# Keys and values as nine rows on 64 partitions, two heads side by side, in a linear-attention and SoLU kernel

## The chip, the cores and the metric

One core of one Trainium2 chip runs the whole program. The metric is the device time of one execution in microseconds (us), the median over several runs. Of the core's engines the text uses short names: PE (TensorE, matrix products), DVE (VectorE), ACT (ScalarE), POOL (GpSimd) and SP (SyncE, whose queue issues every load, store and DMA transpose of this kernel). PSUM is the memory into which PE writes; it has eight banks of 512 float32 columns on 128 partitions.

## What is computed

q, k and v have the shape (8, 8, 576, 64): batches, heads, rows, columns, all float32. Attention is linear: the softmax of q runs along its 64 columns, the softmax of k along the 576 rows.

```python
q_s = softmax(q, axis=-1)                  # along the 64 columns
k_s = softmax(k, axis=2)                   # along the 576 rows
kv  = einsum('bhsd,bhse->bhde', k_s, v)    # 64 x 64 for each head
x   = einsum('bhsd,bhde->bhse', q_s, kv)   # then to (4608, 512)
h   = x @ w_in                             # w_in 512 x 1024
solu = h * softmax(h)
ln  = (solu - mean) / sqrt(var + 1e-6) * g_ln
out = ln @ w_out                           # w_out 1024 x 512
```

w_in, w_out and g_ln come as float64, two 32-bit words a number, and are turned into float32 on the chip. The maximum and the sum in the softmax of k run over rows, and rows lie on partitions; that is why the maxima take a detour over PE, below.

## The kernel before

**Steps and the order list.** The program is a set of Python generators, each of which issues the instructions of one piece of work up to its next `yield`. The string ORDER names the generators one after the other; each name runs one step. `K3*2` is two steps of the keys of batch 3; `.v` puts that step's movable instruction on DVE instead of its usual engine. An engine carries out its instructions in the order in which they were issued, so the list fixes the order on each engine, and on SP's queue the order of the loads. The names: LQ, LK and LV load q, k and the remaining rows of v; V loads and copies a quarter of a batch's v (`V02`: batch 0, quarter 2); K is the keys; Qa, Qb, Qc and R are the softmax of q and its transposes; S a scale; x, h and o are, for each of 36 row tiles of 128 rows, attention, the first and the second product of the feed-forward part; w and y decode the weights; W and Z scale them into two float16 parts; LG loads g_ln; P issues four products whose result nobody reads.

**Row tiles.** A batch's 576 rows are 4 x 128 "main" rows, laid as (p c) with four neighbouring rows on one partition, and 64 "rest" rows. The rest rows of an even batch lie on partitions 0 to 63 and those of the odd batch after it on 64 to 127, and for q two batches share one tile for them.

**Keys (generator `keys`, L354 to L428).** For a batch, `km` holds the main rows of k as [128, 8 heads, 4, 64] and `kr` the rest as [64 of 128, 8 heads, 64]. DVE takes the maxima over the four rows of a partition in two halves of the heads (L365, L367) and joins kr to them (L370). `tops_of` turns the [128, 512] result with four PE transposes into `turned` (L341), reduces it on DVE to a column (L344), spreads the column with four PE transposes into `wide` (L348), and ACT copies that to `kb` (L351). Then kb is subtracted from km in two halves (L376, on POOL or DVE) and from kr (L381), and ACT takes exponentials (L378, L383). PE multiplies: for each pair of heads and each of the four rows two products of 128 rows, 64 columns of weights and 65 moving columns (L395), and 16 products of 64 rows for the rest (L400). The 65th column of v is all ones, so it gives the softmax's denominator. The two heads of a pair write the two halves of the output's partitions, all in one PSUM bank, `kv`. DVE divides (L403 to L407) and takes the largest value (L409), which PE and DVE spread over the partitions (L173, L176), and ACT and DVE write the scaled float16 high and low parts into `bd` (L422 to L426).

**Attention and feed-forward.** `attend` (L529) multiplies bd by the transposed softmax of q, and ACT and DVE copy x out as two float16 parts (L541, L543). `hidden` makes 24 products (L566) into two PSUM banks, and DVE, ACT and POOL work on them for the SoLU and the normalisation (L573 to L622); `project` makes 24 products (L640) for a row tile and copies them out (L648, L650).

**PSUM.** The tag `h` has two places of two banks, `o` one bank, and `att` three banks. turned, wide, kv, x and, in the last six row tiles, every second o take turns in `att`.

**v.** `load_v` loads two heads, [128, 2, 4, 64], and copies them into `vm` beside the ones (ACT, or DVE with `.v`); the rest rows are loaded straight into `vr`. **g_ln** is loaded with one number to a packet, as [128, 8] (L295).

Of the kernel before, what the change touches and what calls it, by code (L numbers as in the profile page):

```python
# [760 lines left out]
```

## Time and profile before

| what | value |
|---|---|
| median of 3 runs | 469.29 us (468.37 to 469.74) |
| profiled execution | 468.76 us, its span 467.0 us |
| granted clock of PE, mean | 0.996 |
| busy: PE, DVE, ACT, POOL | 439.9, 349.9, 282.4, 200.0 us |
| o products L640 | 888 |
| h products L566 | 840 |
| products of k and v, L395 and L400 | 512 and 128 |
| loads of km, kr, vr for one batch, issue to landing | 7.1, 6.2, 4.8 us (medians) |
| DMA packets | 159240, of them 127840 under 512 bytes |

How to read it: a "span" is from the first to the last instruction; the profiled execution's own time is 1.8 us longer. A row of a timeline names start, length, engine, line, operation, output<-inputs, shapes and count. A product's recorded length includes its way through the array, and neighbours overlap, so what a run of products takes is read from its first start to the next one's. A row of groups gives count, busy time, mean length in ns, and the idle time of the engine ahead of it. A row of waits gives who waited for whom, the sum, the number and the longest.

### The profile page before, as it was taken

What the parts mean: (1) busy time and instruction counts of PE and PEld (TensorE: products, weight loads), DVE (VectorE), ACT (ScalarE), POOL (GpSimd) and SP (SyncE); (2) the same over time, 40 slices, a digit from 0 to 9 for tenths busy, and PEclk for the clock granted to TensorE, in tenths of its full rate; (3) what the DMA queues carried; (4) which work ended last, traced back from release to release, by engine and by line L of the source; (5) the groups of instructions that cost most, each with busy time, mean ns of one, the idle gap of its engine ahead of it and who ended that gap; (6) DMA issues with size and microseconds to landing.
All of it is one profiled execution on the core that took longest, in us unless ns stands there. A gap on an engine that the chain in (4) does not pass through costs nothing.

```text
span 467.0 us, 8294 instructions
## 1 busy us (share of the span) xinstructions
PE 439.9 (94%) x3142; PEld 221.4 (47%) x3142; DVE 349.9 (75%) x620; ACT 282.4 (60%) x469; POOL 200.0 (43%) x286
## 2 busy tenths in 40 slices
PE   0678889999999999999999999999999999999997
PEld 0334344455546454545454455445545445444445
DVE  4989999998987889879789788668877844633500
ACT  1789899777658657466667448654764454522401
POOL 4123966577159356314665322735364421211200
PEclk9989999999999999999999999999999999999999
DMA  8999989589593997598757973869324673232522
GB/s 251 311 316 303 208 190 214 104 215 207 152 237 72 219 231 159 146 193 212 146 126 210 226 141 63 226 146 201 71 67 46 135 163 54 60 70 71 133 63 67
DMA packets 159240, 74.99 MB, mean 161 GB/s; under 512 B 127840, under 2 KB 152672, under 8 KB 159200
## 3 DMA queue, kind: packets, MB, share of 16 engines
q1 hardware_dynamic: 159200, 74.47, 69.0%
q8 instruction: 24, 0.39, 0.4%
q14 instruction: 16, 0.13, 0.1%
HBM read 36.70 MB, written 9.44 MB: 99 GB/s over the span
## 4 chain that ended last, share of the span: by engine, by line
PE 86%; DVE 6%; POOL 3%; ACT 3%; DMA 1%; issue 1%; SPq 0%; POOLq 0%; ACTq 0%; DVEq 0%
PE o L640 40%; PE h L566 36%; PE x L529 3%; PE kv L395 3%; PE warm_up L696 1%; DMA qm<-in_q_dram 1%; PE kv L400 1%; DVE wi L289 1%; DVE qnmx L443 1%; POOL qm L445 1%; PE turned L341 1%; PE wide L348 1%; DVE iw L262 1%; POOL km L376 1%; DVE km L376 0%
## 5 line engine op out<-in xcount | busy, mean ns | idle before, releaser
L640 PE MATMUL o<-wo,uT 128*128 128x512 f16 (+1 forms) x888 | 197.4, 373 | 0.0
L566 PE MATMUL h<-wi,xT 128*128 128x512 f16 x840 | 193.1, 379 | 2.7 <-ACT e L609 2.3
L640 PEld LDWEIGHTS <-uT 128*128 128x128 f16 x888 | 86.2, 98 | 97.8 <-issue 0.3
L566 PEld LDWEIGHTS <-xT 128*128 128x128 f16 x840 | 81.5, 98 | 98.8 <-issue 3.0
L573 DVE TENSOR_REDUCE top<-h 128x1 f32<-128x1024 f32 x36 | 43.9, 1221 | 24.9 <-PE h L566 24.7
L602 DVE SCALAR_TENSOR_TENSOR u<-h,nmu,u 128x1024 f16<-128x1024 f32 x36 | 46.0, 1277 | 16.7 <-ACT u L600 16.5
L609 ACT ACTIVATE e<-h,nmu 128x1024 f32<-128x1024 f32 x36 | 40.1, 1113 | 22.1 <-DVE u L602 22.1
L595 DVE SCALAR_TENSOR_TENSOR h<-h,ph,e 128x1024 f32<-128x1024 f32 x36 | 46.3, 1287 | 5.5 <-POOL ph L592 4.0
L589 POOL TENSOR_TENSOR p<-pi,mone 128x1 f32<-128x1 f32 x36 | 25.9, 718 | 49.5 <-DVE pi L586 42.7
L600 ACT ACTIVATE u<-h,nmu 128x1024 f16<-128x1024 f32 x36 | 40.0, 1112 | 0.8
L579 ACT ACTIVATE e<-h,nm,hs 128x1024 f32<-128x1024 f32 x31 | 37.2, 1201 | 0.7
L597 ACT ACTIVATE nmu<-s 128x1 f32<-128x1 f32 x36 | 7.3, 202 | 49.4 <-DVE h L595 49.3
L445 POOL TENSOR_TENSOR qm<-qm,qnmx 128x1024 f32<-128x1024 f32 (+1 forms) x14 | 25.7, 1844 | 21.7 <-DVE qnmx L443 14.6
L650 ACT ACTIVATE os<-o,rr 128x512 f32<-128x512 f32 (+1 forms) x23 | 15.3, 667 | 31.1 <-PE o L640 24.4
L622 POOL TENSOR_TENSOR r<-var,mhalf 128x1 f32<-128x1 f32 x36 | 24.2, 675 | 22.5 <-DVE var L619 22.0
L461 POOL TENSOR_TENSOR qhl<-qm,qhl 128x1024 f16<-128x1024 f32 (+1 forms) x11 | 22.5, 2041 | 19.4 <-DVE qhl L163 10.3
L575 ACT ACTIVATE nm<-top,hs 128x1 f32<-128x1 f32 x31 | 9.1, 294 | 35.2 <-DVE top L573 35.0
L456 POOL TENSOR_TENSOR qm<-qm,qrec 128x1024 f32<-128x1024 f32 (+1 forms) x11 | 20.7, 1879 | 19.2 <-DVE qrec L454 19.1
L543 DVE SCALAR_TENSOR_TENSOR xT<-x,xT 128x512 f16<-128x512 f32 x35 | 23.6, 683 | 5.2 <-ACT xT L541 5.1
L586 POOL TENSOR_SCALAR pi<-am 128x1 f32<-128x1 f32 x19 | 7.5, 393 | 41.8 <-DVE am L583 41.1
L443 DVE TENSOR_REDUCE qnmx<-qm 128x16 f32<-128x1024 f32 (+1 forms) x17 | 19.3, 1147 | 6.0 <-DMA qm<-in_q_dram 6.0
L541 ACT ACTIVATE xT<-x 128x512 f16<-128x512 f32 x35 | 20.0, 590 | 5.9 <-PE x L529 5.8
(139 smaller groups left out, 547.4 us busy)
## 6 DMA issues: line engine op xcount, KB each, us to landing
v<-in_v_dram SPq DMA_DIRECT2D x32, 256.0 KB, 3.7
out_dram<-os SPq DMA_DIRECT2D x31, 256.0 KB, 3.4
km<-in_k_dram SPq DMA_DIRECT2D x7, 1024.0 KB, 7.1
qm<-in_q_dram SPq DMA_DIRECT2D x7, 1024.0 KB, 6.8
w_in<-in_moe_w_in_dram SPq DMA_DIRECT2D x8, 512.0 KB, 6.9
w_out<-in_moe_w_out_dram SPq DMA_DIRECT2D x8, 512.0 KB, 5.6
out_dram<-os SPq DMA_DIRECT2D x10, 128.0 KB, 2.7
qm<-in_q_dram SPq DMA_DIRECT2D x2, 512.0 KB, 4.4
```

The source lines that it names most:

```text
L443: nc.vector.tensor_reduce(shaped(nmx), x, axis=AX.X, op=ALU.max, negate=True)
L445: on(nc.gpsimd).tensor_tensor(x, x, wide(nmx), op=ALU.add)
L566: nc.tensor.matmul(h[:, ns], xT[:, t, kc], wi[:, s, kc, ns], start=(i == 0), stop=(i == len(terms) - 1))
L573: nc.vector.tensor_reduce(top, h, axis=AX.X, op=ALU.max, negate=True)
L579: nc.scalar.activation(e, h, AF.Exp, bias=nm, scale=hs, accum_out=z)
L589: nc.gpsimd.tensor_tensor(p, pi, mone, op=ALU.pow)
L595: nc.vector.scalar_tensor_tensor(h, h, ph, e, op0=ALU.mult, op1=ALU.mult, accum_out=s1)
L600: nc.scalar.activation(u[:, 0], h, AF.Identity, bias=nmu)
L602: nc.vector.scalar_tensor_tensor(u[:, 1], h, nmu, u[:, 0], op0=ALU.add, op1=ALU.subtract)
L609: nc.scalar.activation(e, h, AF.Square, bias=nmu, accum_out=s2)
L622: nc.gpsimd.tensor_tensor(r, var, mhalf, op=ALU.pow)
L640: nc.tensor.matmul(o, uT[:, j, f], wo[:, s, f, cols], start=(f == 0 and j == 0 and s == 0), stop=(f == NF - 1 and j == 1))
```

## The change

k and v are no longer split into main and rest rows. A head's 576 rows lie as nine rows on each of 64 partitions, and an even and an odd head lie beside each other on the two halves of the 128 partitions; for one pair of heads that is one run of [128, 9 x 64] numbers, 2304 bytes to a partition. The loads of kr and vr (the generators LV) go.

The maxima over the nine rows take three steps on DVE (rows 0 to 3 with 4 to 7, then pairs, then the last pair and the ninth row), for batch 0 in two parts, for the others at once. turned and wide are two transposes each; the reduction gives one maximum for each head half, and a new copy (`cols`) spreads it over 64 columns before the second transpose. The subtraction and the exponential run in two parts of [128, 2, 9, 64]. The products are 72 of 64 rows by 64 weight columns by 65 moving columns, in fours that cover the four quarters of the array, and the two row halves write two PSUM banks of the tag `att`. The denominators and the division take two instructions each. The heads' places in `bd` move from pairs (n j) to (i n). g_ln is loaded as eight rows of 128 numbers and turned on PE. A batch's K has 24 steps instead of 28 (batch 0: 27), and P has 9 instead of 11. ORDER is another list throughout, and `.v` stands at other steps; its text is left out here but for the places that the prediction speaks of.

```diff
@@ ORDER
-    "LQ0*2 Q0a*2 LK0*3 Q0b.v Q0c.v Q0a.v Q0b V03 K0.v w3 Q0a w3 K0 Q0a.v Q0a K0*2 Q0b V03 Q0c.v*2 V00 w0 "
-    "K0 w3 Q0b.v K0 w0 Q0a.v K0*2 LV0 P V02.v V00 K0 w3 V01 Q0a P w3 K0.v w0 K0 K0.v w2 w0 V02 w2 w0 P w1 "
-    "K0 V01 K0.v K0 Q0b w1 w3 K0*2 w2 Q0b.v K0 LK1 w0 Q0c K0 w2 K0 P Q0b K0 Q0b w1 LK1 K0 P K0 w2 w1 P y0 "
...
+    "LQ0*2 Q0a*2 LK0 Q0a.v Q0c.v Q0b.v Q0a K0 Q0b.v V00 Q0b V03 Q0c LK0 w3 K0.v V00 Q0a.v w3 Q0a K0*2 V03 "
+    "w3 Q0b K0 K0.v w3 w0 V01.v K0*2 Q0c.v w0 K0*2 V01 K0 P Q0a V02.v Q0b.v Q0a w3 K0.v w0 V11.v w2 K0.v "
+    "w0 K0.v w0 V02 Q0c K0 w2 Q0c P Q0b K0*2 w0 V11 K0 P w3 K0*2 Q0b K0 w1 w2*2 K0 w1 w2 LK1 w1 K0 w1 P "
...
+    "h25 h25.v x28 R7 K7 h22 K7.v h25.v h25 h22 h25.v h28 h25 o21.v Q7a h25 h25.v K7 R7.v o21.v*2 h25 h28 "
...
@@ load_v, load_keys
+    def heads_on_halves(src, b):
+        return src[b].rearrange("(n r) (p c) d -> (r p) n (c d)", r=2, c=KC)
...
+        t = sb.tile([P, KC, D], F32, name=f"v{b}_{i}", tag="v", bufs=2)
+        nc.sync.dma_start(out=t.rearrange("p c d -> p (c d)"), in_=heads_on_halves(v, b)[:, i])
...
+            nc.sync.dma_start(out=km[:, ns].rearrange("p n c d -> p n (c d)"), in_=heads_on_halves(k, b)[:, ns])
...
-        load_rest("kr", k, b)
...
@@ load_gain
-        nc.sync.dma_start(out=gl, in_=g_ln.rearrange("(f p) -> p f", p=P))
+        nc.sync.dma_start(out=rows, in_=g_ln.rearrange("(f p) -> f p", p=P))
+        yield
+        turned = ps.tile([P, NF], F32, name="turned_gl", tag="att", bufs=3)
+        nc.tensor.transpose(turned, rows, ident[0:NF, 0:NF])
...
@@ tops_of
-        turned = ps.tile([P, NP, P], F32, name=f"turned{b}", tag="att", bufs=3)
-        for i in range(NP):
+        turned = ps.tile([P, 2, P], F32, name=f"turned{b}", tag="att", bufs=3)
+        for i in range(2):
             nc.tensor.transpose(turned[:, i], flat[:, i * P : (i + 1) * P], ident)
...
+        col = sm.tile([P, 2, 2], F32, name=f"col{b}", tag="col", bufs=1)
+        nc.vector.tensor_reduce(col, turned.rearrange("p i (r k) -> p i r k", r=2), axis=AX.X, op=ALU.max)
+        yield
+        cols = sm.tile([P, 2, 2, D], F32, name=f"cols{b}", tag="cols", bufs=1)
+        cast(on(nc.scalar), cols, col.unsqueeze(3).broadcast_to([P, 2, 2, D]))
...
@@ keys
+        parts = [slice(m, NP, 2) for m in range(2)]
...
+        for ns in parts if b == 0 else [slice(0, NP)]:
+            nc.vector.tensor_tensor(half[:, ns], km[:, ns, 0 : KC // 2], km[:, ns, KC // 2 : KC - 1], op=ALU.max)
+            yield
+            nc.vector.tensor_tensor(half[:, ns, 0:2], half[:, ns, 0:2], half[:, ns, 2:4], op=ALU.max)
+            yield
+            nc.vector.tensor_tensor(top[:, ns], half[:, ns, 0], half[:, ns, 1], op=ALU.max)
+            nc.vector.tensor_tensor(top[:, ns], top[:, ns], km[:, ns, KC - 1], op=ALU.max)
+            yield
...
+        banks = [ps.tile([P, 512], F32, name=f"kv{b}_{r}", tag="att", bufs=3) for r in range(2)]
+        kv = banks[0]
+        accs = [t[:, 0 : NP // 2 * (D + 1)].rearrange("p (m d) -> p m d", d=D + 1) for t in banks]
...
+        for m in range(2):
+            for c in range(KC):
+                for r, i in ((0, 0), (1, 1), (0, 1), (1, 0)):
+                    o, half, n = accs[r][HALVES[i], m], HALVES[r], 2 * i + m
+                    nc.tensor.matmul(
+                        o, km[half, n, c], vm[half, n, c], start=(m == 0 and c == 0), stop=(m == 1 and c == KC - 1)
+                    )
+            yield
...
+        for r, acc in enumerate(accs):
+            wide = rec[:, r::2].unsqueeze(2).broadcast_to([P, NP // 2, D])
+            nc.vector.tensor_tensor(kvn[:, r::2], acc[:, :, 0:D], wide, op=ALU.mult)
...
-        places = t.rearrange("p s (n j) d -> p s n j d", j=2)
+        places = t.rearrange("p s (i n) d -> p s n i d", i=2)
```

More of the change, by code (lines that the diff above doesn't have):

```diff
@@ L118, in linear_attention_solu_ffn @@
     R = S - SM
-    assert R == 64 and D == 64 and DM == NP * P and B % 2 == 0
+    KC = S // D
+    assert R == 64 and D == 64 and S == KC * D and DM == NP * P and H == 2 * NP and B % 2 == 0
     QS = 2.0**14
@@ L137, in linear_attention_solu_ffn @@
     isc = cst.tile([P, 1], F32, name="isc")
-    vm = cst.tile([P, H, C, D + 1], F32, name="vm")
-    vr = cst.tile([P, H, D + 1], F32, name="vr")
+    vm = cst.tile([P, NP, KC, D + 1], F32, name="vm")
     nc.vector.memset(vm[:, :, :, D : D + 1], 1.0)
-    nc.vector.memset(vr[:, :, D : D + 1], 1.0)
     bd = [cst.tile([P, 2, H, D], F16, name=f"bd{i}") for i in range(3)]
@@ L201, in load_main @@
         nc.sync.dma_start(out=raw[name][:, hs], in_=main_of(src, b)[:, hs])
+    HALVES = slice(0, D), slice(D, P)
+    def heads_on_halves(src, b):
+        return src[b].rearrange("(n r) (p c) d -> (r p) n (c d)", r=2, c=KC)
     def load_v(b, i):
-        hs = slice(i * H // 4, (i + 1) * H // 4)
-        t = sb.tile([P, H // 4, C, D], F32, name=f"v{b}_{i}", tag="v", bufs=2)
-        nc.sync.dma_start(out=t, in_=main_of(v, b)[:, hs])
+        t = sb.tile([P, KC, D], F32, name=f"v{b}_{i}", tag="v", bufs=2)
+        nc.sync.dma_start(out=t.rearrange("p c d -> p (c d)"), in_=heads_on_halves(v, b)[:, i])
         yield
-        cast(on(nc.scalar), vm[:, hs, :, 0:D], t)
+        cast(on(nc.scalar), vm[:, i, :, 0:D], t)
     def load_rest(name, src, b):
         j = b % 2
-        if name == "vr":
-            t = vr[:, :, 0:D]
-        elif j == 0:
-            t = raw[name] = sb.tile([P, H, D], F32, name=f"{name}{b}", tag=name, bufs=1)
-        else:
-            t = raw[name]
+        if j == 0:
+            raw[name] = sb.tile([P, H, D], F32, name=f"{name}{b}", tag=name, bufs=1)
+        t = raw[name]
         nc.sync.dma_start(out=t[j * R : (j + 1) * R], in_=src[b, :, SM:S, :].rearrange("h s d -> s h d"))
@@ L223, in load_keys @@
         parts = 2 if b == 0 else 1
+        km = raw["km"] = sb.tile([P, NP, KC, D], F32, name=f"km{b}", tag="km", bufs=1)
         for i in range(parts):
-            load_main("km", k, b, i, parts)
+            ns = slice(i, NP, parts)
+            nc.sync.dma_start(out=km[:, ns].rearrange("p n c d -> p n (c d)"), in_=heads_on_halves(k, b)[:, ns])
             yield
-        load_rest("kr", k, b)
     def load_queries(b):
@@ L294, in load_gain @@
     def load_gain():
-        nc.sync.dma_start(out=gl, in_=g_ln.rearrange("(f p) -> p f", p=P))
+        rows = cst.tile([NF, P], F32, name="gl_rows")
+        nc.sync.dma_start(out=rows, in_=g_ln.rearrange("(f p) -> f p", p=P))
[3 more added lines that the diff above has]
+        yield
+        nc.vector.tensor_copy(gl, turned)
     def weight_out(i):
@@ L336, in tops_of @@
     def tops_of(top, b):
-        flat = top.rearrange("p h d -> p (h d)")
-        turned = ps.tile([P, NP, P], F32, name=f"turned{b}", tag="att", bufs=3)
-        for i in range(NP):
+        flat = top.rearrange("p n d -> p (n d)")
+        turned = ps.tile([P, 2, P], F32, name=f"turned{b}", tag="att", bufs=3)
+        for i in range(2):
             nc.tensor.transpose(turned[:, i], flat[:, i * P : (i + 1) * P], ident)
         yield
-        col = sm.tile([P, NP], F32, name=f"col{b}", tag="col", bufs=1)
@@ L344, in tops_of @@
-        nc.vector.tensor_reduce(col, turned, axis=AX.X, op=ALU.max)
+        col = sm.tile([P, 2, 2], F32, name=f"col{b}", tag="col", bufs=1)
+        nc.vector.tensor_reduce(col, turned.rearrange("p i (r k) -> p i r k", r=2), axis=AX.X, op=ALU.max)
         yield
-        wide = ps.tile([P, NP, P], F32, name=f"wide{b}", tag="att", bufs=3)
-        for i in range(NP):
-            nc.tensor.transpose(wide[:, i], col[:, i : i + 1].broadcast_to([P, P]), ident)
+        cols = sm.tile([P, 2, 2, D], F32, name=f"cols{b}", tag="cols", bufs=1)
@@ L349, in tops_of @@
+        cast(on(nc.scalar), cols, col.unsqueeze(3).broadcast_to([P, 2, 2, D]))
         yield
-        kb = sb.tile([P, H, D], F32, name=f"kb{b}", tag="kb", bufs=1)
-        nc.scalar.copy(kb.rearrange("p h d -> p (h d)"), wide.rearrange("p n k -> p (n k)"))
+        wide = ps.tile([P, 2, P], F32, name=f"wide{b}", tag="att", bufs=3)
+        for i in range(2):
+            nc.tensor.transpose(wide[:, i], cols[:, i].rearrange("p r k -> p (r k)"), ident)
+        yield
+        kb = sb.tile([P, NP, D], F32, name=f"kb{b}", tag="kb", bufs=1)
@@ L352, in tops_of @@
+        nc.scalar.copy(kb.rearrange("p n d -> p (n d)"), wide.rearrange("p i k -> p (i k)"))
         yield kb
     def keys(b):
-        rows = slice(b % 2 * R, (b % 2 + 1) * R)
         km = raw["km"]
-        parts = 2
-        n = H // parts
-        heads = [slice(p * n, (p + 1) * n) for p in range(parts)]
-        top = sb.tile([P, H, D], F32, name=f"ktop{b}", tag="ktop", bufs=1)
-        half = sb.tile([P, n, 2, D], F32, name=f"khalf{b}", tag="kb", bufs=1)
-        for hs in heads:
-            nc.vector.tensor_tensor(half, km[:, hs, 0:2], km[:, hs, 2:4], op=ALU.max)
+        parts = [slice(m, NP, 2) for m in range(2)]
@@ L366, in keys @@
+        top = sb.tile([P, NP, D], F32, name=f"ktop{b}", tag="ktop", bufs=1)
+        half = sb.tile([P, NP, KC // 2, D], F32, name=f"khalf{b}", tag="khalf", bufs=1)
+        for ns in parts if b == 0 else [slice(0, NP)]:
+            nc.vector.tensor_tensor(half[:, ns], km[:, ns, 0 : KC // 2], km[:, ns, KC // 2 : KC - 1], op=ALU.max)
             yield
-            nc.vector.tensor_tensor(top[:, hs], half[:, :, 0], half[:, :, 1], op=ALU.max)
+            nc.vector.tensor_tensor(half[:, ns, 0:2], half[:, ns, 0:2], half[:, ns, 2:4], op=ALU.max)
@@ L368, in keys @@
             yield
-        kr = raw["kr"]
-        nc.vector.tensor_tensor(top[rows], top[rows], kr[rows], op=ALU.max)
-        yield
+            nc.vector.tensor_tensor(top[:, ns], half[:, ns, 0], half[:, ns, 1], op=ALU.max)
+            nc.vector.tensor_tensor(top[:, ns], top[:, ns], km[:, ns, KC - 1], op=ALU.max)
+            yield
         for kb in tops_of(top, b):
             yield
-        for p, hs in enumerate(heads):
-            wide = kb[:, hs].unsqueeze(2).broadcast_to([P, n, C, D])
-            on(nc.gpsimd).tensor_tensor(km[:, hs], km[:, hs], wide, op=ALU.subtract)
+        for ns in parts:
+            wide = kb[:, ns].unsqueeze(2).broadcast_to([P, NP // 2, KC, D])
+            on(nc.gpsimd).tensor_tensor(km[:, ns], km[:, ns], wide, op=ALU.subtract)
@@ L377, in keys @@
             yield
-            nc.scalar.activation(km[:, hs], km[:, hs], AF.Exp)
+            nc.scalar.activation(km[:, ns], km[:, ns], AF.Exp)
             yield
-            if p == 0:
-                on(nc.gpsimd).tensor_tensor(kr[rows], kr[rows], kb[rows], op=ALU.subtract)
-                yield
-                nc.scalar.activation(kr[rows], kr[rows], AF.Exp)
-                yield
-        kv = ps.tile([P, 512], F32, name=f"kv{b}", tag="att", bufs=3)
-        acc = kv[:, 0 : NP * (D + 1)].rearrange("p (n d) -> p n d", n=NP)
@@ L390, in keys @@
-        for hs in heads:
-            for h in range(hs.start, hs.stop, 2):
-                for c in range(C):
-                    for i in range(2):
-                        o = acc[i * D : (i + 1) * D, h // 2]
-                        nc.tensor.matmul(o, km[:, h + i, c], vm[:, h + i, c], start=(h == 0 and c == 0), stop=False)
-            yield
-        for h in range(0, H, 2):
-            for i in range(2):
-                o = acc[i * D : (i + 1) * D, h // 2]
-                nc.tensor.matmul(o, kr[rows, h + i], vr[rows, h + i], start=False, stop=(h == H - 2))
@@ L402, in keys @@
         den = sm.tile([P, NP], F32, name=f"den{b}", tag="den")
-        nc.vector.tensor_scalar(den, acc[:, :, D], 1e-9, None, op0=ALU.add)
         rec = sm.tile([P, NP], F32, name=f"rec{b}", tag="rec")
+        for r, acc in enumerate(accs):
+            nc.vector.tensor_scalar(den[:, r::2], acc[:, :, D], 1e-9, None, op0=ALU.add)
         nc.vector.reciprocal(rec, den)
         kvn = sb.tile([P, NP, D], F32, name=f"kvn{b}", tag="kb", bufs=1)
-        nc.vector.tensor_tensor(kvn, acc[:, :, 0:D], rec.unsqueeze(2).broadcast_to([P, NP, D]), op=ALU.mult)
+        for r, acc in enumerate(accs):
+            wide = rec[:, r::2].unsqueeze(2).broadcast_to([P, NP // 2, D])
+            nc.vector.tensor_tensor(kvn[:, r::2], acc[:, :, 0:D], wide, op=ALU.mult)
@@ L700, in linear_attention_solu_ffn @@
     works["P"] = warm_up()
-    works["LG"] = call(load_gain)
+    works["LG"] = load_gain()
     for t, row_tile in enumerate(tiles):
@@ L707, in linear_attention_solu_ffn @@
         works[f"LK{b}"] = load_keys(b)
-        works[f"LV{b}"] = call(load_rest, "vr", v, b)
         for i in range(4):
```

1 line of the change is left out of this document (removed), and 139 rows, old and new, of the table ORDER.

## The prediction

> **What bounds the kernel now.** I read the page first (busy shares, chain), then the busy time by windows, then what TensorE (PE) waited for before and after 73 us, then PE's timeline around the steps that the change rewrites. From the page, parts 1 and 4:
>
> ```profile
> PE 439.9 (94%) x3142; PEld 221.4 (47%) x3142; DVE 349.9 (75%) x620; ACT 282.4 (60%) x469; POOL 200.0 (43%) x286
> ...
> PE 86%; DVE 6%; POOL 3%; ACT 3%; DMA 1%; issue 1%; SPq 0%; POOLq 0%; ACTq 0%; DVEq 0%
> ```
>
> PE carries 86% of the chain that ended last. A share of 94% is still an average; the windows show two stages:
>
> ```profile
> 12.00:36.00 24.00, 17.86 (x141) 9.15 (x142) 21.86 (x42) 19.06 (x29) 4.38 (x3) 0.93 1.09 315
> 36.00:56.00 20.00, 16.79 (x108) 8.11 (x107) 19.46 (x24) 17.61 (x26) 12.43 (x9) 1.00 1.09 258
> 56.00:73.20 17.20, 14.98 (x163) 8.17 (x162) 15.92 (x34) 16.87 (x30) 11.02 (x16) 1.00 0.86 198
> 73.20:120.00 46.80, 46.79 (x331) 23.31 (x332) 43.38 (x76) 37.28 (x63) 31.68 (x43) 1.00 0.79 176
> ...
> 300.00:400.00 100.00, 100.00 (x674) 48.97 (x673) 70.17 (x128) 53.77 (x92) 38.76 (x56) 1.00 0.57 115
> ```
>
> (Columns: stretch and length, then busy us of PE, PE's weight loads, DVE, ACT and POOL, each with its count, granted clock, DMA share, GB/s.) Up to 73.2 us PE has holes, while DVE is busy 41.3 of the 44 us from 12 to 56 and the DMA engines are full (share 1.09). From 73.2 us on PE is never free. PE's waits, for the first 76 us and then for 73 us to the end, agree:
>
> ```profile
> PE turned L341 <- DVE ktop L370: 14.4, 1, 14.4
> PE kv L173 <- DVE mx L409: 2.8, 2, 1.4
> PE h L566 <- ACT e L609: 2.3, 3, 1.5
> ```
>
> ```profile
> PE h L566 <- ACT e L609: 0.4, 1, 0.4
> ```
>
> One wait of 0.4 us in 390 us. So in the second stage each microsecond of PE work taken away is a microsecond of the time, as long as DVE (43.4 of 46.8 us just after 73, less later) and ACT still deliver. In the first stage a shorter PE helps little; DVE and the loads set it.
>
> **The change, PE's part.** Batches 2 to 7 have their k and v work after 73.2 us; batches 0 and 1 lie in the first stage. What the rewritten steps take of PE is read from start to start, because the modelled matmul lengths overlap:
>
> ```profile
> 119.71 0.69 PE L529 MATMUL x<-qTr,bd 128*64 128x64 f16 x32
> 120.24 1.06 PE L529 MATMUL x<-qT,bd 128*64 128x128 f16 x32
> 121.23 1.04 PE L640 MATMUL o<-wo,uT 128*128 128x512 f16 x4
> ...
> 285.80 1.10 PE L395 MATMUL kv<-vm,km 128*64 128x65 f32 x32
> 286.73 0.67 PE L529 MATMUL x<-qTr,bd 128*64 128x64 f16 x32
> 287.24 1.13 PE L395 MATMUL kv<-vm,km 128*64 128x65 f32 x32
> 288.30 0.68 PE L400 MATMUL kv<-vr,kr 64*64 64x65 f32 x16
> 288.91 1.47 PE L640 MATMUL o<-wo,uT 128*128 128x512 f16 x6
> ```
>
> The first 32 products of k and v take 286.73 - 285.80 = 0.93 us, 29 ns each; the other 32 take 1.06 us; the 16 of the rest rows take 0.61 us. Together 2.60 us a batch. Two neighbours write different halves of the output partitions; 29 ns each is 58 ns a pair. The 16 of the rest rows are 8 pairs, 0.47 us at 58 ns, so 0.14 us more goes on entering and leaving the 64-row form, and the 32 ahead of them took 0.13 us more than the first 32 (part of this is the change of form, too). I book 0.23 us for each entry and exit.
>
> The Trainium skill (TensorEngine Tiling, Key Properties) says that a change of tiling mode, not of the tile, drains TensorE. The rows agree, and it speaks against the change, which has two such entries a batch instead of one. By that rule and by the rows the booking is the same.
>
> After, a batch has 72 products of 64 rows and 65 columns, in fours on the four quarters of the array (row half by column half), each four into two PSUM banks. If a four runs as a pair does now, 18 fours take 18 x 58 ns = 1.05 us, with two entries (the two parts are separate steps) 1.5 us. That is 1.1 us less a batch; six batches, **-6.5 us**. The bounds: the old pace of 29 ns a product gives 72 x 29 ns + 0.46 = 2.55 us, no gain; no overlap at all gives 72 x 58 ns + 0.46 = 4.6 us, a loss of 2.0 us a batch. I take the fours: pairs already run side by side with separate weights and separate data, and the 32 products x<-qTr above start 16.6 ns apart (0.53 us), so PE can take in products and their weight loads at the rate that the fours need (14.6 ns each).
>
> The k maxima are turned and spread by transposes on PE, four each a batch before, two each after:
>
> ```profile
> 330.75 0.60 PE L341 MATMUL turned<-ident,ktop 128*128 128x128 f32 x4
> 331.18 1.46 PE L640 MATMUL o<-wo,uT 128*128 128x512 f16 x6
> 332.48 0.60 PE L348 MATMUL wide<-ident,col 128*128 128x128 f32 x4
> 332.91 0.81 PE L566 MATMUL h<-wi,xT 128*128 128x512 f16 x3
> ```
>
> Four take 0.43 us, so 0.43 us a batch goes; six batches, **-2.6 us**. The bounds are narrow, since the form stays the same. The transpose for g_ln (one, below 0.11 us by these rows) falls in the first stage among other waits and costs nothing there.
>
> **Vector, scalar, GpSimd and loads.** The rows for the k work:
>
> ```profile
> L365 DVE TENSOR_TENSOR khalf<-km 128x512 f32<-128x512 f32 x16 | 12.1, 754 | 0.1
> L376 DVE TENSOR_TENSOR km<-km,kb 128x1024 f32<-128x1024 f32 x8 | 10.6, 1330 | 0.2 <-ACT kb L351 0.2
> ...
> L367 DVE TENSOR_TENSOR ktop<-khalf 128x256 f32<-128x256 f32 x16 | 6.6, 416 | 0.1
> L344 DVE TENSOR_REDUCE col<-turned 128x4 f32<-128x512 f32 x8 | 5.5, 688 | 1.8 <-PE turned L341 1.8
> L370 DVE TENSOR_TENSOR ktop<-ktop,kr 64x512 f32<-64x512 f32 x8 | 5.4, 676 | 0.1
> ```
>
> ```profile
> L376 POOL TENSOR_TENSOR km<-km,kb 128x1024 f32<-128x1024 f32 x8 | 18.9, 2359 | 1.7 <-ACT kb L351 1.5
> ...
> L381 POOL TENSOR_TENSOR kr<-kr,kb 64x512 f32<-64x512 f32 x5 | 6.3, 1265 | 2.6 <-ACT kb L351 2.5
> ```
>
> Maxima on DVE: before 2 x 754 + 2 x 416 + 676 = 3.0 us; after one of 1024 elements (some 1.4 us by the row of 512), one of 512 and two of 256, 3.0 us again. The reduction of the turned maxima has half the elements (-0.3 us); the second denominator and the second normalisation give that back. The subtractions grow from 1024 to 1152 elements (POOL 2.36 to about 2.65 us, DVE 1.33 to about 1.5), and those of the rest rows go. The new order puts 13 of the 16 on POOL instead of 8: DVE loses 8 x 1.33 - 3 x 1.5 = 6 us, POOL gains 13 x 2.65 - 8 x 2.36 - 5 x 1.27 = 9 us of its 267 idle us. On ACT the rest's exponential goes, the main ones and the copies of v grow by an eighth, and the column copy `cols` is new: about level. None of that is on PE's path after 73 us. What hides it is the h and o products that the order lists between the steps; where that cover is missing, PE stands for the engine's time.
>
> The new wait: the two kv banks hold two of the three places with the tag att from the first product of k and v until the maxima are read, where one was held before. Queued behind such a wait on PE is everything, since it works in order. The tightest place that I find in the new list is "x28 R7 K7": the transposes of batch 7 need a place soon after x28, whose two copies out cost 0.59 and 0.68 us:
>
> ```profile
> L543 DVE SCALAR_TENSOR_TENSOR xT<-x,xT 128x512 f16<-128x512 f32 x35 | 23.6, 683 | 5.2 <-ACT xT L541 5.1
> ...
> L541 ACT ACTIVATE xT<-x 128x512 f16<-128x512 f32 x35 | 20.0, 590 | 5.9 <-PE x L529 5.8
> ```
>
> One full miss is 1.3 us; I book **+0.5 us** for all of them, bounds 0 and 6 x 1.3 = 8 us.
>
> First stage: k comes as whole rows of 2304 bytes and the separate loads of kr and vr go. For batches 0 and 1, DVE saves its 676 ns and half of 688 ns less about 0.3 us for the split steps, some 0.7 us each; with the subtractions about level I book **-1 us**. Bounds: -3 us, if PE's own saving of 1.5 us in both batches counts there; +4 us, because on SP's queue V11 (0.29 MB, 1 us at the 315 GB/s of the window) now stands ahead of w2 and w1, w1's last load is listed behind some 3 us more of DVE work than before, and 8 fewer filler products (P) may leave the clock low for longer (0.93 in the window from 12 to 36 us).
>
> **Sum.** -6.5 - 2.6 + 0.5 - 1 = -9.6 us. The profiled execution took 468.76 us (span 467.0 and 1.8 around it), so 459.2; the median of the runs is 0.5 us above it, so **459.7 us**. About 0.3% (1.4 us) is what a measurement of this kernel can tell from no change.
>
> **Rivals.**
> *The pace stays at 29 ns a product* (the quarters do not run four abreast, or the taking in of products is the limit). For: the 32 products x<-qT above take 0.99 us, 31 ns each, nearly the same pace in another form. Against: the 16.6 ns of x<-qTr. Then kv gains nothing and -2.6 - 1 + 0.5 remains: 466.2 us. The Trainium skill (TensorE: Matmul & The Clock Gate, Back-to-back issue gap) gives a floor of about 25 ns from start to start; by it 72 products would be an estimated 1.8 us and the time some 2 us lower than in this rival; the 16.6 ns speak against it here.
> *No overlap across row halves: slower.* Successive products of a four switch the row half every time, which no product in this trace does. If each switch makes PE finish the product before, a batch takes 4.6 us instead of 2.6: +12 us for six batches, -2.6 - 1 + 0.5: 478 us. It decides from (2.60 + 0.43 us) / 72, about 42 ns a product less the entries (36 ns): above that the kernel is slower. Against: products in different column halves do overlap.
> *The gain is given back in waits*: the first stage ends 4 us later, or the att places make PE stand at several batches: 459.7 + 5 = 465 us, and up to no change if both.
>
> **How the numbers follow.** Forecast (456 to 462.5) 0.63; old pace 0.14; given back in waits 0.15, two fifths of it within 0.3% of before; slower 0.07, with a little for a first stage that loses over 10 us; better than 456 0.01. Faster 0.87, same 0.06, slower 0.07. The range runs from 455 (first stage -3 us, and no att wait, 457, with 2 us for the unseen order) to 466.5, which takes in the old pace.
>
> **What would show it.** Right: 72 products of k and v in 1.4 to 1.6 us a batch from start to start; turned and wide x2 in 0.22 us; PE without idle time from about 72 us on, one or two waits of about 1 us on xT or on kv's maxima at most. Wrong: products of k and v at 29 ns or more each, PE idle before turned, x or kv after 75 us, or PE filled only several microseconds later than 73.2 us.

## The result

The changed kernel took 475.32 us (median of 4 executions, 472.68 to 476.62) against 468.83 us before (468.14 to 469.74): ratio 1.0130, 95% interval 1.0106 to 1.0155. It is 6.5 us slower, where 9.1 us less than this median of before was forecast. The page's parts 1 and 4 of the changed kernel's first profiled execution (472.68 us, span 470.8 us):

```profile
PE 435.9 (93%) x3615; PEld 216.1 (46%) x3615; DVE 343.3 (73%) x605; ACT 283.5 (60%) x473; POOL 208.1 (44%) x301
...
PE 77%; DMA 7%; ACT 6%; DVE 6%; issue 2%; POOL 0%; SPq 0%; ACTq 0%; DVEq 0%
```

PE is busy 4 us less, but the chain of waits that ended last lies on PE for 77% instead of 86%: DMA (7%) and ACT (6%) have come in. The windows, cut as in the prediction, and what PE waited for from 73 us to the end:

```profile
12.00:36.00 24.00, 13.72 (x184) 7.39 (x185) 21.92 (x45) 20.01 (x30) 4.27 (x3) 0.88 1.01 310
36.00:56.00 20.00, 19.94 (x118) 9.34 (x117) 18.85 (x24) 17.92 (x27) 11.18 (x8) 0.97 0.87 242
56.00:73.20 17.20, 14.39 (x225) 7.65 (x224) 16.42 (x38) 16.40 (x29) 9.06 (x12) 1.00 0.88 175
73.20:120.00 46.80, 41.72 (x349) 20.24 (x347) 38.02 (x69) 31.12 (x51) 28.48 (x37) 0.96 0.58 132
```

```profile
PE o L640 <- ACT os L650: 5.1, 1, 5.1
PE x L529 <- DMA qT<-qhl: 1.1, 1, 1.1
PE h L566 <- ACT e L609: 0.2, 1, 0.2
```

In the fourth window PE was busy 46.79 of 46.80 us before; now 5.1 us are missing, and the granted clock is 0.96 instead of 1.00. The timeline of PE shows where, and also what the new products take:

```profile
59.30 2.33 PE L395 MATMUL kv<-vm,km 64*64 64x65 f32 x144
61.56 1.04 PE L696 MATMUL warm_up<-bd 128*128 128x512 f16 x4
...
77.81 5.34 PE L640 MATMUL o<-wo,uT 128*128 128x512 f16 x24
88.24 2.16 PE L640 MATMUL o<-wo,uT 128*128 128x512 f16 x5 [5.08 <-ACT os L650]
```

**The hole.** Behind the 24 products of the first row tile (o0) PE stands for 5.08 us, until ACT has copied o0 out of PSUM (os, L650): the tag o has one bank, and the list has the products of o1 next. The copy is late because ACT, which works in order, has four other things ahead of it. ACT in the changed kernel, then in the kernel before:

```profile
82.76 0.20 ACT L597 ACTIVATE nmu<-s 128x1 f32<-128x1 f32 x1 [0.66 <-DVE h L595]
83.00 1.11 ACT L600 ACTIVATE u<-h,nmu 128x1024 f16<-128x1024 f32 x1
84.01 0.59 ACT L541 ACTIVATE xT<-x 128x512 f16<-128x512 f32 x1
85.46 1.11 ACT L609 ACTIVATE e<-h,nmu 128x1024 f32<-128x1024 f32 x1 [0.87 <-DVE u L602]
...
86.57 1.03 ACT L158 CAST qhl<-qm 128x1024 f16<-128x1024 f32 x1
87.50 0.69 ACT L650 ACTIVATE os<-o,rr 128x512 f32<-128x512 f32 x1
```

```profile
82.96 0.69 ACT L650 ACTIVATE os<-o,rr 128x512 f32<-128x512 f32 x1 [0.90 <-PE o L640]
83.55 0.20 ACT L597 ACTIVATE nmu<-s 128x1 f32<-128x1 f32 x1
```

Before, ACT stood ready 0.90 us ahead of the end of o0 and copied at once; four products of h lay between o0 and o1 on PE:

```profile
73.21 4.48 PE L566 MATMUL h<-wi,xT 128*128 128x512 f16 x20 [0.41 <-ACT e L609]
77.52 5.34 PE L640 MATMUL o<-wo,uT 128*128 128x512 f16 x24
82.70 1.03 PE L566 MATMUL h<-wi,xT 128*128 128x512 f16 x4
83.70 5.34 PE L640 MATMUL o<-wo,uT 128*128 128x512 f16 x24
```

In the new list the copy comes behind the first part of the normalisation of h3 (nmu, u), a copy of x, a square that waits for DVE (L609, written to the buffer of e), and a cast.

**The half clock behind it.** Busy time by windows of 2 us; the last column but two is the granted clock:

```profile
86.00:88.00 2.00, 0.00 (x0) 0.00 (x0) 2.00 (x4) 2.00 (x4) 1.26 (x4) 1.00 0.72 140
88.00:90.00 2.00, 1.76 (x5) 0.68 (x5) 2.00 (x3) 1.67 (x4) 1.53 (x1) 0.60 0.64 122
90.00:92.00 2.00, 2.00 (x6) 0.69 (x5) 1.59 (x4) 0.00 (x0) 1.65 (x5) 0.54 0.66 128
92.00:94.00 2.00, 2.00 (x11) 0.88 (x9) 0.00 (x0) 0.00 (x0) 0.00 (x0) 1.00 1.05 181
```

5 and 6 products in 2 us instead of 11: from 88.4 to 91.8 us the clock is half, and eight products take 0.43 us instead of 0.216, 1.7 us more. The Trainium skill (TensorE: Matmul & The Clock Gate, What's actually happening) says that the clock falls to half after an idle window of about 3.4 us and needs a busy one to come back; the rows agree.

**The products of k and v.** 61.56 - 59.30 = 2.26 us a batch, not the forecast 1.5. The group has 1152 records for 8 x 72 = 576 products:

```profile
L395 PE MATMUL kv<-vm,km 64*64 64x65 f32 x1152 | 19.6, 224 | 0.0
```

Each float32 product leaves two records. The prediction (and the table of the kernel before, 512 and 128) counted records as products, and the 16 products that "The kernel before" gives for the rest rows are eight products with 16 records.

### The profile page after: what moved, and what is told of

It is laid out like the page before. It is cut to its first block, busy times and chain, and to the rows that moved or that the text cites. A ratio compares the mean times of both kernels' runs of the same rounds, so it can differ in the third digit from the quotient of the medians.

```text
span 470.8 us, 9221 instructions
## 1 busy us (share of the span) xinstructions
PE 435.9 (93%) x3615; PEld 216.1 (46%) x3615; DVE 343.3 (73%) x605; ACT 283.5 (60%) x473; POOL 208.1 (44%) x301
## 4 chain that ended last, share of the span: by engine, by line
PE 77%; DMA 7%; ACT 6%; DVE 6%; issue 2%; POOL 0%; SPq 0%; ACTq 0%; DVEq 0%
PE o L640 37%; PE h L566 32%; DMA qT<-qhl 3%; PE x L529 3%; PE kv L395 2%; DMA w_in<-in_moe_w_in_dram 2%; PE h L558 2%; DMA qm<-in_q_dram 1%; DVE u L602 1%; ACT e L579 1%; ACT junk_out L311 1%; ACT wo L333 1%; DVE khalf L370 1%; DVE h L595 1%; ACT qhl L158 1%
## 5 line engine op out<-in xcount | busy, mean ns | idle before, releaser
L640 PE MATMUL o<-wo,uT 128*128 128x512 f16 (+1 forms) x888 | 199.7, 376 | 5.1 <-ACT os L650 5.1
L566 PEld LDWEIGHTS <-xT 128*128 128x128 f16 x840 | 81.6, 98 | 97.1 <-issue 2.0
L583 POOL TENSOR_SCALAR am<-nm 128x1 f32<-128x1 f32 x23 | 9.9, 431 | 110.6 <-ACT nm L575 110.6
L609 ACT ACTIVATE e<-h,nmu 128x1024 f32<-128x1024 f32 x36 | 40.1, 1113 | 14.4 <-DVE u L602 14.3
L381 POOL TENSOR_TENSOR km<-km,kb 128x1152 f32<-128x1152 f32 x13 | 34.7, 2667 | 8.3 <-ACT kb L359 8.1
L579 ACT ACTIVATE e<-h,nm,hs 128x1024 f32<-128x1024 f32 x31 | 37.2, 1200 | 0.7
L650 ACT ACTIVATE os<-o,rr 128x512 f32<-128x512 f32 (+1 forms) x23 | 15.4, 669 | 31.3 <-PE o L640 20.5
L589 POOL TENSOR_TENSOR p<-pi,mone 128x1 f32<-128x1 f32 x36 | 21.7, 603 | 24.2 <-DVE pi L586 22.3
L622 POOL TENSOR_TENSOR r<-var,mhalf 128x1 f32<-128x1 f32 x36 | 21.8, 607 | 10.9 <-DVE var L619 10.3
L529 PE MATMUL x<-qT,bd 128*64 128x128 f16 x512 | 18.8, 223 | 6.2 <-ACT bd L424 3.8
L456 POOL TENSOR_TENSOR qm<-qm,qrec 128x1024 f32<-128x1024 f32 x9 | 17.1, 1902 | 16.7 <-DVE qrec L454 13.5
```

The costliest lines, as they stand in the source:

```text
L381: on(nc.gpsimd).tensor_tensor(km[:, ns], km[:, ns], wide, op=ALU.subtract)
L529: nc.tensor.matmul(acc[j * D : (j + 1) * D, pr, cols], t[:, s, 2 * pr + j], qT[:, 2 * pr + j, cols], start=(s == 0), stop=(s == 1),)
L566: nc.tensor.matmul(h[:, ns], xT[:, t, kc], wi[:, s, kc, ns], start=(i == 0), stop=(i == len(terms) - 1))
L579: nc.scalar.activation(e, h, AF.Exp, bias=nm, scale=hs, accum_out=z)
L609: nc.scalar.activation(e, h, AF.Square, bias=nmu, accum_out=s2)
L640: nc.tensor.matmul(o, uT[:, j, f], wo[:, s, f, cols], start=(f == 0 and j == 0 and s == 0), stop=(f == NF - 1 and j == 1))
```

## The experiments

Each median stands with its number of executions, and its ratio is to the kernel before in the same series (468.6 to 469.2 us). The theory after the first trace: the layout is good, and the new list loses the time, by the hole. The rivals: the layout's own longer chain loses it, or the clock, for want of fillers. First, which half of the change is slow.

**The new layout under the old list** (places moved at five spots, where the two kv banks would not have fitted):

```diff
-    "LQ0*2 Q0a*2 LK0 Q0a.v Q0c.v Q0b.v Q0a K0 Q0b.v V00 Q0b V03 Q0c LK0 w3 K0.v V00 Q0a.v w3 Q0a K0*2 V03 "
+    "LQ0*2 Q0a*2 LK0*2 Q0b.v Q0c.v Q0a.v Q0b V03 K0 w3 Q0a w3 K0*2 Q0a.v Q0a K0*2 Q0b V03 Q0c.v*2 V00 w0 K0 "
...
```

> New layout with the old order list (steps that no longer exist left out, the new ones put beside their neighbours; five places moved because the two kv banks would not fit). Theory A, the list: the layout saves PE 0.33 us a batch in the k and v products (2.26 for 2.59 us) and 0.43 us in the transposes, six batches 4.6 us, and the loss comes from the new list, which lets PE run dry at the first o product; then about 464 us, and no idle time of PE above 1 us after 75 us. Rival B, the layout: two banks of three, longer subtractions and twice the k and v records cost more than they save; then 472 us or more with waits of PE before turned, x or kv.

Measured: 474.96 us (4), ratio 1.0127 (1.0090 to 1.0164). PE's waits after 73 us:

```profile
PE h L563 <- ACT e L606: 2.2, 2, 1.7
PE wide L353 <- ACT cols L155: 1.4, 1, 1.4
PE h L563 <- issue: 0.7, 1, 0.7
```

No hole behind o0, and a granted clock of 1.000, but several waits where before had one of 0.4 us: the longer chain turned, col, cols (on ACT), wide does not fit the cover that the old list gave it. The expected 464 us were missed by 11 us; the time is where the rival put it, with a wait ahead of wide, though hardly any ahead of turned, x or kv.

**The old layout under the new list** (khalf in a buffer of its own, so that the list fits):

```diff
-        half = sb.tile([P, n, 2, D], F32, name=f"khalf{b}", tag="kb", bufs=1)
+        half = sb.tile([P, n, 2, D], F32, name=f"khalf{b}", tag="khalf", bufs=1)
```

> Old layout with the new order list (the old steps put back beside their neighbours, the loads of the rest rows right behind the last load of k and the last copy of v; khalf has a buffer of its own, else the list cannot be followed). Theory A, the list: some 4.6 us more than the changed kernel, about 480 us, with a hole of about 5 us in PE after the first o. Rival B, the layout: about 469 us, no such hole.

Measured: 483.69 us (4), ratio 1.0305 (1.0260 to 1.0350). PE's timeline has the hole again:

```profile
82.06 5.34 PE L635 MATMUL o<-wo,uT 128*128 128x512 f16 x24
92.47 6.75 PE L635 MATMUL o<-wo,uT 128*128 128x512 f16 x24 [5.07 <-ACT os L645]
```

So the hole comes with the list, whatever the layout; and under the new list, which was written for the new layout, that layout is 8.4 us faster than the old.

**The copy of o0 earlier in the list:**

```diff
-h3.v x4 Q1c.v h3*2 o0 h3 x4 o0 Q1c o0.v*2 Q1c h2.v o1 h2 o0 h5.v
+h3.v x4 o0*5 Q1c.v h3*3 x4 Q1c*2 h2.v o1 h2 h5.v
```

> The changed kernel; in the list only the four product steps and the copy of o0 are moved, ahead of h3's second pass on DVE and its square on ACT. Theory A1, the hole of 5.1 us comes from the copy of the first o standing behind h3's chain on ACT, while o has one bank: the hole falls to about 2 us, the half-clock stretch behind it goes, and the time falls by 3 to 5 us, to about 471 us. Rival A2, PE has nothing to do there whatever the copy does (DVE feeds it too late): the hole only moves behind the second o or to the next h, and the time stays at 474 to 476 us.

Measured: 470.72 us (10), ratio 1.0032 (1.0003 to 1.0060). The hole shrank and no half clock followed:

```profile
87.61 5.34 PE L638 MATMUL o<-wo,uT 128*128 128x512 f16 x24 [2.23 <-ACT os L648]
```

**One row half after the other:**

```diff
-            for c in range(KC):
-                for r, i in ((0, 0), (1, 1), (0, 1), (1, 0)):
+            for r in range(2):
+                for c in range(KC):
+                    for i in range(2):
```

> The changed kernel; the k and v products go through one row half at a time, so neighbours share the row half and only column halves differ. Theory: four products on four quarters run side by side (their records start 7 ns apart, 58 ns a four of records). Then pairs take twice as long: about 4.3 us a batch for 2.26, and six batches make the kernel some 12 us slower, about 487 us. Rival: PE takes in one record each 15.7 ns whatever quarter it goes to; then 2.26 us a batch as before and no change.

Measured: 485.06 us (2), ratio 1.0337 (1.0290 to 1.0383). PE's timeline of batch 2 in this kernel, then in the changed one:

```profile
116.47 3.91 PE L396 MATMUL kv<-vm,km 64*64 64x65 f32 x144
120.31 1.04 PE L567 MATMUL h<-wi,xT 128*128 128x512 f16 x4
```

```profile
112.30 2.33 PE L395 MATMUL kv<-vm,km 64*64 64x65 f32 x144
114.56 1.04 PE L566 MATMUL h<-wi,xT 128*128 128x512 f16 x4
```

3.84 us in pairs, 2.26 in fours, from start to start: the four quarters do run beside each other, at 116 ns a four of products (18 fours are 2.09 us; about 0.17 us are left for entering and leaving). The Trainium skill (TensorEngine Tiling, Key Properties) says that different tiles work independently; these rows agree.

**Four more fillers** (P), three behind the fourth, one behind x0, against the half clock of the first stage:

```diff
-w1 P K0 w1
+w1 P*4 K0 w1
...
-w1 x0 y0 x0
+w1 x0 P y0 x0
```

> The changed kernel with four more filler steps P (16 products that nobody reads): three right behind the fourth P, where PE stands 2.9 us ahead of the first x, and one behind the first x. Theory C, the clock: the changed kernel's PE is idle enough in the first stage to keep its clock at half for 6.8 us and more, in unprofiled runs longer than in the profiled one (mean clock 0.978 against 0.989), which costs 2 to 3 us; then one low stretch of at most 3.4 us in the first 70 us and about 472 us. Rival: the low clock lies where PE waits anyway and costs nothing; then 475 us.

Measured: 477.38 us (4), ratio 1.0177 (1.0143 to 1.0211), 2 us worse; the hole was still 5.0 us. The mean clock was 0.986 to 0.993 in these executions, 0.978 to 0.989 in the changed kernel's, so there was less half clock and still more time. The theory that the missing fillers cost the time fell.

**o1 in another bank.** Only row tile 1 takes its place from att:

```diff
-            o_tag = "att" if t >= LATE and (t + i) % 2 else "o"
+            o_tag = "att" if t == 1 or t >= LATE and (t + i) % 2 else "o"
```

> The changed kernel, list untouched; only the second row tile's o takes its PSUM place from the tag att instead of the one bank of o. Theory A1 (one bank of o and a late copy): the hole of 5.1 us behind the first o falls to under 1 us, with the half-clock stretch behind it gone, and the time falls by 5 to 7 us, to 469 us or below. Rival A2 (DVE feeds PE too late, the copy is only the first to show it): a hole of 3 us or more comes back at the next h or o, and the time stays above 472 us.

Measured: 467.89 us (10), ratio 0.9970 (0.9946 to 0.9993), 7.4 us less than the changed kernel. On PE, o0 and o1 are now one run:

```profile
78.84 10.52 PE L640 MATMUL o<-wo,uT 128*128 128x512 f16 x48
89.20 3.62 PE L566 MATMUL h<-wi,xT 128*128 128x512 f16 x16
```

With the four fillers as well:

> Both: the four fillers and the second o in att. If the hole and the low clock are the two costs of the changed kernel beyond what its layout saves on PE (4.4 us), the time is below the kernel before: 464 to 467 us. If the first stage is bound by DVE and the loads, so that both only move the wait, 469 us or more.

Measured: 470.22 us (10), ratio 1.0015 (0.9990 to 1.0039): the fillers cost 2 us here too.

The same edit in the two other kernels, old layout under the new list and the kernel before:

> As e2 (old layout, new list) with the second o in att. If the hole behind the first o belongs to the list, not to the layout, it goes here as it did in e6: some 7 us less than e2's 483.7, about 476.5 us. If not, less than 3 us.

> The kernel before with the second o in att and nothing else. It has no hole there, so no change is expected: within 1 us of 468.8 us. If it gains as e6 did, the place in PSUM and not the list is what counts.

Measured: 477.05 us (4), ratio 1.0181 (1.0157 to 1.0206), 6.6 us less than without it; and 468.62 us (10), ratio 0.9994 (0.9977 to 1.0010), no change. The hole takes both: the new list and one bank.

**The old list, with `cols` moved from ACT to DVE** right behind the reduction, and `wide` put up to 1.7 us of PE's work later:

```diff
-K3*2 h9.v*2 h5 h10 h9.v o4.v K3 Q2c
+K3 K3.v h9.v*2 h5 h10 h9.v o4.v Q2c
...
```

> New layout with the old list as in e1, but the new copy cols on DVE right behind the reduction that feeds it (e1: on ACT), and the second transpose wide moved behind up to 1.7 us more of PE's work where the list leaves room. In e1 PE stood 6.0 us in all after 73 us, 3.4 us of it for cols or for an exponential queued behind cols. Theory: those go, and the time is 3 to 5 us below e1, 470 to 472 us in plain runs. Rival: the waits move on to the next step of the keys; then within 1.5 us of e1's 475 us.

Measured: 471.52 us (10), ratio 1.0060 (1.0033 to 1.0086): 3.4 us less than with cols on ACT, as expected. The wait for cols is gone, but others came:

```profile
PE x L526 <- DVE xT L540: 1.3, 1, 1.3
PE h L563 <- issue: 1.2, 1, 1.2
PE turned L343 <- DVE ktop L372: 0.6, 1, 0.6
PE kv L392 <- DVE xT L540: 0.6, 1, 0.6
```

**The first stage.** With o1 in att, the six steps that write bd of batch 0 go ahead of w1's decode, V11 behind w1 (and, not shown here, the first maxima of batch 1 behind W's first steps):

```diff
-Q0b K0 w1 w2*2 K0 w1 w2 LK1 w1 K0 w1 P K0 w1 K0 Q0b.v w2 K0 V12 K0 w1 x0
+Q0b K0*7 w1 w2*2 w1 V11.v w2 LK1 w1*2 P w1 Q0b.v w2 V12 w1 V11 x0
```

> As e6 (changed kernel, second o in att), and in the list three things of the first stage moved: the six steps that write bd of batch 0 ahead of the last quarter of w_in's decoding (before, ACT held them behind a load of w_in), the load and copy of V11 behind that quarter's loads, and the first maxima of batch 1 behind W's first steps (before, DVE stood for k's load there). Theory: the first stage waits for w_in's last quarter and for k's load, through what is queued behind them; the first x comes 2 to 3 us earlier than at 31.05 us, the first o 1 to 2 us earlier than at 78.8, and the time falls 1 to 2 us below e6's 467.9. Rival: DVE's sum of work sets the first stage; the first x comes earlier, the first o not, and the time stays within 0.7 us of e6.

Then x15 and x21, the two places with a wait for qT, later as well:

```diff
-x15 h12 x15 h12 x14
+h12*2 x14 x15*2
...
-x21 h15.v K5.v h16 x18 x20 h16.v h15 V52 h16 LQ5 h17 x18
+h15.v K5.v h16 x18 x20 h16.v h15 V52 h16 LQ5 h17 x21 x18
```

> As e9, and the products x15 and x21, which stood 0.9 and 1.2 us for a transpose of q in e6, moved behind the next products of the list. Theory: these two waits go, another 1 to 2 us, about 465 us. Rival: another wait takes their place, no change from e9.

Measured: 468.32 us (10), ratio 0.9988 (0.9971 to 1.0005); and 468.76 us (10), 0.9992 (0.9973 to 1.0011). The first x came at 28.4 us instead of 31.0, but PE then waited for w_in's largest value, and o0 started at 81.0 us (78.8 with o1 in att alone):

```profile
PE wide_in L168 <- DVE m_in L276: 5.9, 1, 5.9
```

The last of these kernels has no wait of PE left after 73 us, and is no faster: what the second stage gained, the first one lost.

**The changed kernel again, three more traces.** No edit.

> The changed kernel, unchanged. The mean clock of an execution comes in steps of about 0.0036, which is one stretch of 3.4 us at half clock in 470 us (1.7 / 470). Its profiled execution had 0.989, three stretches, and both places of them are seen; the other three had 0.978, six stretches, and took 1.8 to 3.9 us more. Theory D: the time of an execution follows this count; each further stretch costs up to 1.7 us where PE bounds, less in the first stage. Then over more executions the clock lies between 0.978 and 0.989, and those at 0.989 take 472 to 473 us, those at 0.978 474.5 to 476.6. Rival: the clock and the time are not tied, and executions at one clock spread over the whole 472 to 477.

> The changed kernel, unchanged, for another trace. Theory D: the hole behind the first o (5.1 us) and one stretch of half clock behind it are there again; an execution with a lower mean clock than 0.989 has its further stretches in the first stage, between 30 and 42 us and around 63 to 70 us, where PE has idle pieces of 0.6 to 1.1 us. Rival: they lie behind 92 us, in the part that PE fills.

> The changed kernel, unchanged, for a third trace. As for the second look: the hole of 5.1 us and its stretch are there in every execution, and the first o starts between 77.8 and 80 us, later by what the first stage loses in stretches of half clock; rival: the first o starts at the same time whatever the clock.

Measured: 474.67 us (4), ratio 1.0124 (1.0100 to 1.0147), and single times of 476.76 and 477.09 us. The hole is there each time (5.2 to 5.3 us). The first o starts at 80.89, 81.68 and 81.55 us, later than the 80 us expected at most: the first trace was a lucky one. ACT and PE in the last of them:

```profile
27.21 0.51 ACT L422 ACTIVATE bd<-kvn,s_kv 64x256 f16<-64x256 f32 x1
30.69 1.12 ACT L257 ACTIVATE iw<-w_in 128x1024 f32<-128x1024 f32 x1 [2.97 <-DMA w_in<-in_moe_w_in_dram]
31.83 0.40 ACT L424 COPY bd<-bd 64x256 f16<-64x256 f16 x1
```

```profile
67.86 6.16 PE L566 MATMUL h<-wi,xT 128*128 128x512 f16 x20 [1.14 <-ACT e L609]
...
81.55 5.34 PE L640 MATMUL o<-wo,uT 128*128 128x512 f16 x24
92.14 4.26 PE L640 MATMUL o<-wo,uT 128*128 128x512 f16 x10 [5.25 <-ACT os L650]
```

ACT's last decode of w_in waits for its load, with bd of batch 0, and so the first x, behind it. It starts at 27.79 us before (a wait of 0.29), at 28.85 in the changed kernel's first trace and at 30.7 to 31.6 in the three others; in all four the first x follows 1.6 us behind that start. (In the kernel before the first x comes only at 33.45 us, but fillers keep PE busy up to then.) In this trace PE, idle for 5 us, then runs at half clock from 31 to 41 us, and again around 70 us, where 20 products of h take 6.16 us instead of 4.48. On the tie between clock and time the theory held in part: 468.3 us at clock 1.00 and 470.1 at 0.992 in the kernel before (28 and 19 executions), but the changed kernel's executions at 0.982 and 0.978 overlap (474.4 to 476.8, 474.0 to 477.1).

**What makes that load late?** Three edits of the kernel with o1 in att: V11's load behind the last loads of w_in; w0's decode on DVE ahead of two subtractions, so that a buffer comes free earlier; both.

```diff
-w0 V11.v w2 K0.v w0 K0.v w0 V02
+w0 w2 K0.v w0 K0.v w0 V02
...
-w1 w2 LK1 w1
+w1 w2 V11.v LK1 w1
```

> e6_o1_in_att with one more edit: the load of a quarter of batch 1's v (V11, 0.29 MB) moved on SP's queue behind the last loads of w_in, its copy moved along to just ahead of x0. In nine traces of kernels that keep this list's order of w1 and bd, the first o starts 48.6 to 50.9 us behind ACT's last decode of w_in, which waits for the last load: 27.79 and 77.52 us in before, 28.85 and 77.81 in the changed kernel's lucky execution, 30.7 to 31.6 and 80.9 to 81.7 in three others. Theory L: V11's load ahead of w_in on the DMA engines makes that load late; without it the last decode starts 1 us earlier (29.45 in e6), most of the executions lose one stretch of half clock, and the time falls by 1 to 2 us to 466 to 467. Rival: the load is late for another reason (its buffer comes free late, or the engines are full anyway), and the time stays within 0.7 us of 467.9.

```diff
-w2 K0.v w0 K0.v w0 V02
+w2 w0*2 K0.v*2 V02
```

> e6_o1_in_att with one more edit: the two decode steps of w0 that stand between and behind the two subtractions of batch 0's keys on DVE go ahead of both, so that a buffer of w_in comes free 1.35 to 2.7 us earlier and the last load of w_in is issued that much earlier (at 23.5 us in the changed kernel, 22.6 in before). Theory M: the buffer, held by DVE's decode, sets that load; the last decode starts 1 to 2.5 us earlier, at 27.5 to 28.5 us, as in before, and the time falls by 1 to 2 us to 466 to 467. Against it: the keys of batch 0 come 1.35 to 2.7 us later, and bd and x0 with them, where they are not behind the decode anyway. Rival: the DMA engines are full and the landing doesn't move: within 0.7 us of 467.9, or later if the keys become the bound.

> The edits of e16_v11_later and e17_decode_first together. Theories L and M: 2 to 3 us below e6_o1_in_att's 467.9, at 465 to 466, clearly below before (ratio about 0.993), the first o at 77 to 77.5 us and at most two stretches of half clock. Rival: the first stage is bound by all of its loads and DVE's work and not by this one load: 467 to 468.5.

Measured: 467.93 us (12), ratio 0.9976 (0.9958 to 0.9994); 467.08 us (12), 0.9969 (0.9954 to 0.9984); 467.47 us (12), 0.9968 (0.9952 to 0.9984). V11's load is not it: the median is the same, and the last decode starts at 29.44 us with the edit, 29.45 without. The buffer has a part: with w0's decode first, the last decode starts at 28.71 and 28.75 us (both edits) with no wait. But the time hardly moves: the keys now come later (ACT's first write of bd starts at 28.30 us instead of 27.12), the first x is still at 30.3 us (31.0 without the edit), and o0 starts no earlier (81.1 and 79.4 us in these two traces, 78.8 without). That loads, keys and decode bound the first stage together fits this, but is not shown; which of them must move by how much was not separated further. In nine traces (the changed kernel's four, those of o1 in att and of these three edits of it, and that of the earlier copy of o0) the start of o0 goes with the stretches of half clock (3.4 us each) ahead of it: two where it starts at 77.8 and 78.8 us, three at 79.4, four at 80.0 to 81.7. Whether the stretches cost this time or only mark the waits that do is open. In the trace of both edits, o0 and o1 on PE:

```profile
79.36 10.52 PE L640 MATMUL o<-wo,uT 128*128 128x512 f16 x48
```

## Why the prediction was wrong

The profiles add up if the span is cut at the first product of o (traces; us). The one wait of 0.4 us of the kernel before stands at 73.2 us, ahead of this cut.

| kernel | o0 starts | from there to the end | of it PE's waits and half clock | rest: PE's work |
|---|---|---|---|---|
| before | 77.5 | 389.5 | 0 | 389.5 |
| changed, first trace | 77.8 | 393.0 | 6.2 + 1.7 | 385.1 |
| changed, last trace | 81.6 | 393.6 | 6.6 + 1.9 | 385.1 |
| old layout, new list | 82.1 | 397.6 | 6.6 + 1.4 | 389.6 |
| the same, o1 in att | 82.9 | 391.8 | 2.2 | 389.6 |
| changed, o1 in att | 78.8 | 387.6 | 2.3 | 385.3 |
| the same, V11 later and w0's decode first | 79.4 | 384.8 | 0 | 384.8 |

PE's work after that point is 4.2 to 4.8 us less, not 9.1, in the rows with the new layout; and about 8 us of waits and half clock, and 0.3 to 4.2 us of first stage, were added to the changed kernel. The new layout under the old list is not in the table: from 77.9 us on it takes 392.7 us with 4.0 us of listed waits, which leaves 388.7; where the 3.6 us above 385.1 go was not followed. By the prediction's own steps:

- *PE bounds the kernel after 73 us, so its saving is time.* Right as far as it goes: the last row has no waits, and keeps the whole saving after that point.
- *72 products in 1.5 us a batch, -6.5.* This step failed in size. The 2.60 us before were 40 products with 80 records, 58 ns a pair of records and 65 ns a product; after, 72 products are 144 records in 2.26 us. "Four abreast" was right (58 ns a four of records, 15.7 ns a record, and pairs cost 3.84 us), but a product counts twice. The saving is 2.60 - 2.26 = 0.34 us a batch, -2.0 instead of -6.5 us. (Entering and leaving took about 0.17 us a batch, not the booked 0.46.) With this term alone put right the prediction's sum is -5.1 us, a smaller gain and not a loss. The page could have said so: 512 + 128 records stood beside 8 x (32 + 8) = 320 products in the code.
- *Transposes, -2.6.* Borne out with the term above: -2.0 - 2.6 = -4.6, and the table shows -4.2 to -4.8.
- *Other engines off PE's path, covered by the h and o products that the order lists between.* The busy times came as forecast (DVE -6.6, POOL +8.1, ACT +1.1 us), but the cover failed, and that cost the sign. The list was searched for the K steps' places, and not for the copy of the first o: one bank, and ACT's copy behind four other pieces of work. In the first trace that is 5.1 us of wait and 1.7 us at half clock; giving o1 another bank took 7.4 us off the time.
- *att places, +0.5.* No wait for a place in att showed up in the changed kernel after 73 us; x21's 1.1 us is a wait for a DMA transpose, which the sum had not. Under the old list with cols on DVE, the waits of x and kv for DVE's copy of an x (1.3 and 0.6 us) look like such waits.
- *First stage -1, bounds -3 and +4.* The lucky trace has +0.3, the others +3.4 to +4.2: about the upper bound. Of the reasons given there, DVE's work ahead of the last load of w_in has a part in the late decode, though taking it away brought the first o no earlier; V11's load and the fillers, the other two, are not it.
- *Rivals.* "Gain given back in waits" had the right kind, and its first stage 4 us later came about in three of four traces; but the hole behind o0 was in neither of its places. "No overlap over row halves" fell. "29 ns a product" (no gain from k and v) was nearer to the -2.0 us than the forecast, for a wrong reason: the quarters do run four abreast.

Together, in the first trace: -4.4 of PE's work, +6.2 of waits (hole 5.1, x21 1.1) and +1.7 of half clock are 3.5 us after the first o; with 0.3 us ahead of it 3.8, the whole difference of the spans. The spans of the other three traces are 6.0, 7.9 and 8.2 us longer than before, 3.4 to 4.2 us of it ahead of the first o.

Open is why the last load of w_in lands up to 2.7 us apart between executions of the same kernel, and why four fillers made the kernel slower by 2 us. In both traces with them an x waits once, 1.2 and 1.1 us (at 364 and 356 us), for nothing that the profile shows; the rest of the 2 us has no account.

## What to carry to other kernels

Count the instructions in the code against the records in the trace before costing a product. When a new order is written, follow every tile with one buffer through the in-order engine that frees it: here the first use after a stage change was where the cover was missing. And run a new layout and a new order crosswise, each with the other's old half: here both crosswise kernels were slower than the kernel before, and showed that the hole comes with the list, and that the new layout meets waits of its own under the old one. That the layout saves PE's work was told by cutting the spans, not by the crosswise times.
